# Both heads' scores in one product for the first two units: q stacked, k beside zeros

## The chip, the cores and the metric

The kernel runs on one core of a Trainium2 chip. The metric is device time in microseconds (us): three runs of the kernel before gave a median of 1116.27 us (1116.1 to 1117.86).

## The reference

Attention with two kinds of masks (heads 0 to 3 see 32 keys back, heads 4 to 7 every fourth of 128 back), and a gated feed-forward on the result, with RMS normalisation ahead of it. All is float32.

```
q, k, v: (8 batches, 8 heads, 576 positions, 64)
scores = q k^T / 8, masked by head; attn = softmax(scores) ; out = attn v
x = out as 4608 tokens x 512
xn = x / sqrt(mean(x^2) + 1e-6) * rms_g
y = (silu(xn w_gate) * (xn w_val)) w_out        w_gate, w_val: 512 x 1536, w_out: 1536 x 512
```

## The kernel before, in words

The 4608 tokens are worked off in 16 units of 288 (half a batch each). A unit has four pairs of heads (c = 0 to 3, heads 2c and 2c+1) and 14 bursts: three blocks of 96 queries for each of the first two pairs, four classes of 72 for the other two. A burst is a short chain: TensorE's scores of both heads (`scored`), VectorE's mask and maximum (`scores_max`, L384), ACT's exponentials (L395), sums, POOL's or VectorE's scaling (L411), TensorE's transposes (L487), ACT's copy (L467), TensorE's product with v (L496), ACT's copy into the unit's x (L428). The feed-forward of a unit is 12 groups of gate, value and output products (L650 in float32 for unit 0, L653 and L656 in three parts for the others).

Nothing is scheduled by hardware choice: each engine runs its instructions in the order in which they are written down. Tables of step numbers at the head of the file, and `later(dt, rank, fn)`, which puts a piece of work into a later step, set this order. Unit 0's attention has no other matrix work beside it; filler products (`busy`, L774) stand between its bursts. Unit 1's attention stands inside unit 0's feed-forward, and so on.

SP issues all transfers, in the order of the table ORDER at first: q and k of pairs 0 and 1, v, q and k of pair 2, the first two weight pieces, and so on. The weights come as 64-bit words and are turned into float32 in steps: a rebase on POOL or ACT (L166, L168), then shifts and ors on VectorE (L174, L177, L181). A ninth transfer waits until the first of the eight before it has landed, since eight counters (DMAHW0 to DMAHW7) serve all transfers in turn.

Units 0 and 1 (`u < NNAT`) work their scores in plain float32, with a contraction of 128 rows of which only 64 hold data. `zeros` makes, for each pair of heads, a tile of 128 partitions with q and k of one head beside q and k of the other; it fills partitions 64 to 127 with zeros (L262), and `load_qk` (L273) writes partitions 0 to 63 in one transfer. `scored` then has one product per head (L509). For the second unit's pairs 1 to 3 the zeros are written in later steps (table ZEROS) and the loads are issued in later steps (table SECOND). Unit 2 uses L509 too, with other tiles; from unit 3 on, L512.

## Time and profile before

| | |
|---|---|
| median of three runs | 1116.27 us |
| the profiled execution | 1116.57 us, of it 1114.8 us span |
| PE busy | 1102.5 us, 99% of the span |
| DVE, ACT, POOL busy | 60%, 64%, 61% |
| granted TensorE clock | 1.00 |
| L509, rows of scores | 168, from 5.1 to 152.7 us |
| L262, zeros | 13 on POOL, 3 on DVE, 538 to 680 ns each |

A float32 product shows as two rows, each with its weight load (PEld). PE is TensorE, DVE VectorE, ACT ScalarE, POOL GpSimd; a name with a q, such as SPq, is that engine's sequencer. In the chain of waits a row has start, length and what ran. In the timeline a row has start, length, engine, line, operation, output <- input, shape and how many; in brackets stands the engine's idle time before it, and what ended it. In the rows of groups the last columns are busy time in all and mean ns of one, then the idle time before them. In the rows of transfers the size of one and the median time from issue to landing stand last.

### The profile page before, as it was taken

How to read it: one execution, taken by the hardware profiler on the slowest of the kernel's cores; microseconds unless marked ns; L12 is line 12 of the kernel's file. 1: busy time of each engine (PE TensorE's matmuls, PEld its weight loads, DVE VectorE, ACT ScalarE, POOL GpSimd, SP SyncE). 2: the span in 40 equal slices, each digit the busy share in tenths (PEclk: the TensorE clock that was granted, in tenths of full speed). 3: DMA queues.
4: the chain of work that ended last, by engine and by line, in shares of the span. 5: the costliest groups of instructions: out<-in, count | busy, mean ns of one | idle time of the engine just before them, and what ended most of it. 6: DMA issues, size and time to landing. Idle time of an engine off the chain costs nothing.

```text
span 1114.8 us, 25463 instructions
## 1 busy us (share of the span) xinstructions
PE 1102.5 (99%) x8362; PEld 1076.9 (97%) x8362; DVE 670.9 (60%) x2734; ACT 708.8 (64%) x2579; POOL 674.7 (61%) x1154
## 2 busy tenths in 40 slices
PE   7999999999999999999999999999999999999998
PEld 5787999999999999999999999999999999999998
DVE  7889667656566564656656565665656656565312
ACT  6795676757576675767657576675757667575311
POOL 7423578756586665757657575675658657584211
PEclk9999999999999999999999999999999999999999
DMA  9665213212131121311212121131312212120000
GB/s 252 195 231 197 73 43 88 84 35 79 41 95 50 41 85 41 94 40 55 82 39 84 41 83 54 47 96 29 87 43 80 64 32 80 53 73 13 11 13 22
DMA packets 61542, 82.16 MB, mean 74 GB/s; under 512 B 7298, under 2 KB 41090, under 8 KB 61410
## 3 DMA queue, kind: packets, MB, share of 16 engines
q1 hardware_dynamic: 61410, 80.54, 24.4%
q8 instruction: 66, 1.08, 0.4%
q14 instruction: 66, 0.54, 0.2%
HBM read 71.08 MB, written 9.44 MB: 72 GB/s over the span
## 4 chain that ended last, share of the span: by engine, by line
PE 94%; POOL 2%; ACT 1%; DVE 1%; DMA 1%; issue 1%; SPq 0%; POOLq 0%; ACTq 0%; DVEq 0%
PE acc L656 17%; PE g L656 17%; PE v L656 17%; PE acc L653 9%; PE g L653 8%; PE v L653 8%; PE s L512 3%; PE o L500 3%; PE acc L650 2%; PE v L650 2%; PE g L650 2%; PE t L487 2%; PE o L501 1%; PE g L487 1%; PE o L496 1%; PE s L509 1%
## 5 line engine op out<-in xcount | busy, mean ns | idle before, releaser
L723 POOL TENSOR_TENSOR hlo<-th,hhi 128x288 fp32r<-128x288 f32 x179 | 145.7, 814 | 185.1 <-ACT hhi L722 169.9
L656 PE MATMUL acc<-hhi,lo 128*128 128x288 f32 x720 | 212.6, 295 | 0.0
L698 DVE SCALAR_TENSOR_TENSOR th<-th,g 128x288 f32<-128x288 f32 x180 | 81.8, 454 | 213.0 <-ACT pt L467 124.7
L395 ACT ACTIVATE t<-t,sum 96x128 f32<-96x128 f32 (+3 forms) x448 | 165.3, 372 | 33.5 <-DVE sum L384 32.0
L656 PE MATMUL g<-xhi,lo 128*128 128x288 f32 x612 | 180.3, 295 | 0.0
L656 PE MATMUL v<-xhi,lo 128*128 128x288 f32 x612 | 180.2, 294 | 0.0
L411 POOL TENSOR_SCALAR t<-t,sum 72x72 f32<-72x72 f32 (+3 forms) x414 | 152.2, 379 | 31.6 <-DVE sum L405 20.5
L693 ACT ACTIVATE th<-g 128x288 f32<-128x288 f32 x180 | 73.9, 411 | 151.3 <-PE g L487 59.0
L323 POOL TENSOR_TENSOR vlo<-vt,vhi 128x128 fp32r<-128x128 f32 x182 | 84.2, 463 | 116.7 <-ACT vhi L319 113.5
L656 PEld LDWEIGHTS acc<-hhi,lo 128*128 128x128 f32 x720 | 135.4, 188 | 0.0
L722 ACT CAST hhi<-th 128x288 fp32r<-128x288 f32 x180 | 77.8, 432 | 85.3 <-DVE th L711 84.7
L442 DVE TENSOR_TENSOR xraw<-o,xraw 64x72 f32<-64x72 f32 (+1 forms) x364 | 97.3, 267 | 42.0 <-ACT xraw L431 38.5
L656 PEld LDWEIGHTS v<-xhi,lo 128*128 128x128 f32 x612 | 115.1, 188 | 0.0
L656 PEld LDWEIGHTS g<-xhi,lo 128*128 128x128 f32 x612 | 115.1, 188 | 0.0
L711 DVE TENSOR_TENSOR th<-th,v 128x288 f32<-128x288 f32 x180 | 81.0, 450 | 54.7 <-PE v L656 53.0
L653 PE MATMUL acc<-hhi,hi_o 128*128 128x288 f32 x360 | 109.0, 303 | 0.0
L653 PE MATMUL g<-xhi,hi_g 128*128 128x288 f32 x357 | 106.8, 299 | 0.0
L656 PE MATMUL acc<-hlo,hi_o 128*128 128x288 f32 x360 | 106.4, 296 | 0.0
L431 ACT COPY xraw<-o 64x72 f32<-64x72 f32 (+1 forms) x364 | 95.5, 262 | 9.7 <-PE o L501 7.6
L353 POOL TENSOR_TENSOR ks<-qk,ks 128x288 fp32r<-128x288 f32 (+2 forms) x104 | 93.3, 901 | 3.1
L656 PE MATMUL g<-xlo,hi_g 128*128 128x288 f32 x322 | 95.1, 295 | 0.0
L362 POOL TENSOR_TENSOR qs<-qk,qs 64x288 fp32r<-64x288 f32 x104 | 84.2, 809 | 14.6 <-ACT qs L357 7.8
(188 smaller groups left out, 3522.2 us busy)
## 6 DMA issues: line engine op xcount, KB each, us to landing
qk<-in_qk_dram SPq DMA_DIRECT2D x60, 288.0 KB, 2.9
vt<-in_v_dram SPq DMA_DIRECT2D x196, 64.0 KB, 1.9
qk<-in_qk_dram SPq DMA_DIRECT2D x30, 352.0 KB, 3.0
out_dram<-ot SPq DMA_DIRECT2D x64, 144.0 KB, 1.9
qk<-in_qk_dram SPq DMA_DIRECT2D x30, 304.0 KB, 2.9
raw<-in_w_gate_dram SPq DMA_DIRECT2D x12, 512.0 KB, 5.7
raw<-in_w_val_dram SPq DMA_DIRECT2D x12, 512.0 KB, 5.5
raw<-in_w_out_dram SPq DMA_DIRECT2D x12, 512.0 KB, 4.2
```

Source lines behind the costliest of these rows:

```text
L323: G.tensor_tensor(out=vl, in0=vs.pop(b), in1=vh, op=ALU.subtract)
L353: ek.tensor_tensor(out=ks[:, 1, :nkt], in0=kr, in1=ks[:, 0, :nkt], op=ALU.subtract)
L362: eq.tensor_tensor(out=qs[D:], in0=qr[D:], in1=qs[D:], op=ALU.subtract)
L395: A.activation(out=t[:nq, a, :n], in_=t[:nq, a, :n], func=AF.Exp, scale=-1.0, bias=sm[:nq, a, 0:1], accum_out=sm[:nq, a, 1:2] if u or i % ...
L411: (V if u == 0 and (c, i) > (NC - 1, 0) else G).tensor_scalar(out=t[:nq, a, :n], in0=t[:nq, a, :n], scalar1=sm[:nq, a, 3:4], scalar2=1.0, ...
L431: A.copy(out=to[a * D:(a + 1) * D], in_=o[a * D:(a + 1) * D, (2 + a) * nq:(3 + a) * nq])
L442: V.tensor_tensor(out=to[rows], in0=o[rows, a * nq:(a + 1) * nq], in1=to[rows], op=ALU.add)
L653: PE.matmul(out, wh[:, cc, :], xh, start=start, stop=False)
L656: PE.matmul(out, w[:, cc, :], v, start=False, stop=stop and k == 1)
L698: V.scalar_tensor_tensor(out=t, in0=t, scalar=1.0, in1=g, op0=ALU.add, op1=ALU.mult)
L711: V.tensor_tensor(out=t, in0=t, in1=v_ps[:, :U], op=ALU.mult)
L723: (V if (u, j) == (NU - 1, NJ - 1) else G).tensor_tensor(out=lo, in0=t, in1=hi, op=ALU.subtract)
```

## The change

The tile of a pair of heads now has 288 columns of q and two blocks of k. Partitions 0 to 63 hold q of the first head and partitions 64 to 127 q of the second. The first block of k has the first head's k in partitions 0 to 63 and zeros below; the second has zeros in partitions 0 to 63 and the second head's k below. One product with q stacked as the stationary operand, and both blocks as the moving operand, gives both heads' scores side by side. The zeros cover k's columns alone. The load is three transfers: q and k of the first head (L274), k of the second (L275), q of the second (L276). The host's arrays are as before, and already hold q and k in both halves of the rows.

```diff
-        t = cst.tile([P, 2, U + KW], F32, tag=f"hi{4 * (u * NC + c)}", name=f"qk_{u}_{c}")
+        t = cst.tile([P, U + 2 * KW], F32, tag=f"hi{4 * (u * NC + c)}", name=f"qk_{u}_{c}")
+        ks = t[:, U:].rearrange("p (a k) -> p a k", a=2)
         def fill():
             for a, e in enumerate(engines):
-                e.memset(t[D:, a, :U + geometry(u, c)[2]], 0.0)
+                e.memset(ks[(1 - a) * D:(2 - a) * D, a, :geometry(u, c)[2]], 0.0)
...
-        heads[u, 2 * c], heads[u, 2 * c + 1] = t[:, 0], t[:, 1]
+        heads[u, c] = t[:, :U], ks
         return t

     def load_qk(u, c, t):
         nkt = geometry(u, c)[2]
-        nc.sync.dma_start(out=t[:D, :, :U + nkt],
-                          in_=qk_in[u, 2 * c:2 * c + 2, :D, :U + nkt].rearrange("a p n -> p a n"))
+        nc.sync.dma_start(out=t[:D, :U + nkt], in_=qk_in[u, 2 * c, :D, :U + nkt])
+        nc.sync.dma_start(out=t[D:, U + KW:U + KW + nkt], in_=qk_in[u, 2 * c + 1, D:, U:U + nkt])
+        nc.sync.dma_start(out=t[D:, :U], in_=qk_in[u, 2 * c + 1, D:, :U])
...
             sv = s_ps[:QB].rearrange("q (a t k) -> q a t k", a=2, t=2)
+            if q[0] < NNAT:
+                if a:
+                    return
+                qs, ks = heads[q[0], q[1]]
+                PE.matmul(sv[:nq, :, 0, :n], qs[:, qc:qc + nq], ks[:, :, kc:kc + n], start=True, stop=True)
+                return
             if q[0] < NEX:
```

On SP, at the start of the program, the order before was this (qk_0 to qk_3 are the tiles of unit 0's pairs, raw the weight pieces; what an instruction waits for stands in brackets):

```order
L273 DMA qk_0_103<-in_qk_dram 64x2x576
L273 DMA qk_1_106<-in_qk_dram 64x2x576
L280 DMA v_0_123<-in_v_dram 128x384
L273 DMA qk_2_109<-in_qk_dram 64x2x576
L154 DMA raw_126<-in_w_gate_dram 128x1024
L154 DMA raw_126<-in_w_val_dram 128x1024
L280 DMA v_1_129<-in_v_dram 128x384
L273 DMA qk_3_112<-in_qk_dram 64x2x576
L280 DMA v_3_132<-in_v_dram 72x512 [waits DMAHW0_49]
L280 DMA v_2_134<-in_v_dram 72x512 [waits DMAHW1_49]
L762 DMA gs<-in_rms_g_dram 128x4x1 [waits DMAHW2_49]
L154 DMA raw_137<-in_w_gate_dram 128x1024 [waits DMAHW3_49]
```

With the change SP starts so:

```order
L274 DMA qk_0_103<-in_qk_dram 64x576
L275 DMA qk_0_103<-in_qk_dram 64x288
L276 DMA qk_0_103<-in_qk_dram 64x288
L274 DMA qk_1_106<-in_qk_dram 64x576
L275 DMA qk_1_106<-in_qk_dram 64x288
L276 DMA qk_1_106<-in_qk_dram 64x288
L282 DMA v_0_127<-in_v_dram 128x384
L274 DMA qk_2_109<-in_qk_dram 64x576
L275 DMA qk_2_109<-in_qk_dram 64x288 [waits DMAHW0_49]
L276 DMA qk_2_109<-in_qk_dram 64x288 [waits DMAHW1_49]
L154 DMA raw_132<-in_w_gate_dram 128x1024 [waits DMAHW2_49]
L154 DMA raw_132<-in_w_val_dram 128x1024 [waits DMAHW3_49]
```

The first w_val moves from the sixth to the twelfth place and now waits for the landing of the fourth transfer; before, it waited for none. The second pair of weights moves from the places 12 and 13 to 20 and 21, where it waits for the first w_val (DMAHW3) and the second v (DMAHW4).

On TensorE, in unit 0's feed-forward with unit 1's attention in it, the order before was this (t and g are transposes of L487 or gate products of L650, o the product with v, s the scores):

```order
L487 MATMUL t_1_696<-ident,t_0_2_597 128x96 [waits DVE_49,PE_49]
L487 MATMUL t_1_696<-ident,t_0_2_597 128x96
L496 MATMUL o_0_1_697<-pt_0_1_650,v_0_144 128x192 [waits PE_49,Activation_49]
L650 MATMUL g_2_717<-xn_588,f_539 128x288 [waits DVE_49]
L650 MATMUL g_2_717<-xn_590,f_539 128x288
L650 MATMUL g_2_717<-xn_593,f_539 128x288
L650 MATMUL g_2_717<-xn_595,f_539 128x288
L487 MATMUL g_2_717<-ident,t_1_0_610 128x96 x2
L509 MATMUL s_2_0_722<-qk_2_119 72x104 [waits DMAHW7_49,DVE_49,Pool_49]
L509 MATMUL s_2_0_722<-qk_2_119 72x104 [waits Pool_49]
```

The same place with the change:

```order
L489 MATMUL t_1_692<-ident,t_0_2_596 128x96 [waits DVE_49]
L489 MATMUL t_1_692<-ident,t_0_2_596 128x96
L498 MATMUL o_0_1_693<-pt_0_1_647,v_0_154 128x192 [waits PE_49,Activation_49]
L658 MATMUL g_2_713<-xn_587,f_538 128x288 [waits DVE_49]
L658 MATMUL g_2_713<-xn_589,f_538 128x288
L658 MATMUL g_2_713<-xn_592,f_538 128x288
L658 MATMUL g_2_713<-xn_594,f_538 128x288
L489 MATMUL g_2_713<-ident,t_1_0_608 128x96 x2
L513 MATMUL s_2_0_718<-qk_2_119 72x2x104 [waits DMAHW3_49,DMAHW4_49,DVE_49,DMAHW5_49,PE_49,Pool_49]
```

Two products of scores are one of twice the columns; it waits for three transfers and for TensorE's own counter, which the transposes ahead no longer do. The order of the other work is unchanged on every engine.

## The prediction

> **What bounds the kernel now.** I read the busy times by stage first, because the change touches only the first two units of tokens, whose attention is over by 112 us. A row has the stretch and its length, then busy time and number of instructions of PE, PEld, DVE, ACT and POOL, the granted clock, the DMA share and GB/s.
>
> ```profile
> 0.00:5.00 5.00, 2.50 (x5) 1.49 (x5) 1.61 (x3) 1.58 (x2) 4.37 (x24) 1.00 0.55 126
> 5.00:45.00 40.00, 34.41 (x208) 26.37 (x209) 32.99 (x147) 27.72 (x110) 24.82 (x40) 1.00 0.92 240
> 45.00:112.00 67.00, 67.00 (x333) 53.92 (x332) 60.04 (x130) 50.69 (x144) 22.42 (x18) 1.00 0.60 211
> ```
>
> From 45 to 112 us TensorE is busy all 67.00 us: there only shorter matrix work shortens the run. Before 45 us it is idle for 2.50 + 5.59 us, and its busy time holds filler products (L774) that nobody waits for. There the chain of waits decides, which I read next, in that window.
>
> ```profile
> 0.73 0.73 SPq L273
> ...
> 4.07 7.11 DMA raw<-in_w_val_dram
> ...
> 11.33 1.11 POOL f L166
> 12.44 0.86 POOL t L411
> ...
> 32.04 0.70 POOL qk L262 x2
> ...
> 35.17 0.88 POOL rst L568
> ...
> 43.30 2.21 PE v L650 x8
> ```
>
> The chain starts in the DMA queue: the first pair of weight pieces is complete when w_val lands at 4.07 + 7.11 = 11.18 us, and POOL's rebase L166 starts on it at 11.33. Behind that instruction POOL holds the softmax scaling L411, for which TensorE's transposes wait. From there the chain runs over all four engines, with no slack that I can name, to 43.30, where TensorE becomes full. I therefore count a delay at 11.33 as a delay of the end, one for one.
>
> **The change, part by part.**
>
> *Products.* There are 28 bursts (14 in each of two units) with two products each, which become one with twice the columns and the same stationary width. Does a product cost its columns or its weight load? Three pieces of the chain from a stretch where TensorE has no gap, and one group of weight loads:
>
> ```profile
> 45.84 0.44 PE s L509 x4
> 46.27 1.94 PE acc L650 x8
> ...
> 50.84 0.36 PE s L509 x4
> L509 PEld LDWEIGHTS s<-qk x39: 141/143/165, 45.5 to 111.9; 128*72 128x72 f32 x32, 128*96 128x96 f32 x7
> ```
>
> A product is two rows here. The first four rows have 128 columns each: 0.44 / 512 = 0.86 ns a column. The last four have 104: 0.36 / 416 = 0.87. Weight products have 288: 1.94 / 2304 = 0.84. The rows of 104 columns follow each other every 90 ns although one weight load takes 143, so loads are overlapped and columns set the pace. Two rows of 256 columns cost 512 x 0.84 to 0.86 = 0.43 to 0.44 us against 0.44: 0 to 0.01 us a burst. About ten bursts (39 loads / 4) lie in the full stretch, a gain of 0 to 0.1 us; I take 0.1. Earlier, TensorE waits anyway.
>
> [...] The rows above grow by 0.08 us for 96 columns, 0.83 ns a column, which leaves nothing fixed to save.
>
> VectorE loses nothing by waiting for a whole burst, as it did so before: its first read started when the fourth row had ended (33.47 + 0.60 = 34.07), not after the second.
>
> ```profile
> 33.47 0.60 PE L509 MATMUL s<-qk 128*96 128x128 f32 x4
> 34.11 0.29 DVE L384 CUSTOM_DVE_ANT_0 t<-s,mask 96x128 f32<-96x128 f32 x1
> ```
>
> In many bursts the new product also waits for TensorE's own counter. What it waits for stands 5 to 14 products earlier, and the old order has such waits ahead of output products in the full stretch; I cost them at nothing. Without that cover each would cost about the drain behind a last row, 0.60 (the busy time of four rows, below) - 0.44 = 0.16 us, and ten of them 1.6.
>
> *Fills.* Each now leaves out q's columns.
>
> ```profile
> L262 POOL MEMSET qk<- 64x576 f32 x5 | 2.6, 573 | 0.1
> L262 POOL MEMSET qk<- 64x704 f32 x4 | 2.6, 679 | 0.1
> 8.02 1.36 POOL L411 TENSOR_SCALAR t<-t,sum 96x96 f32<-96x96 f32 x4 [1.96 <-DVE sum L384]
> 11.33 1.11 POOL L166 TENSOR_SCALAR f<-raw 128x1024 f32<-128x1024 f32 x1 [0.83 <-DVE sum L384]
> 17.83 1.13 POOL L166 TENSOR_SCALAR f<-raw 128x1024 f32<-128x1024 f32 x1 [0.28 <-DVE sum L405]
> 34.93 0.16 DVE L567 TENSOR_SCALAR rst<-rps 96x3 f32<-96x3 f32 x1
> 46.31 2.37 POOL L171 TENSOR_SCALAR raw<-raw 128x1024 f32<-128x1024 f32 x1 [7.65 <-issue]
> ```
>
> From 573 and 679 ns one column costs (679 - 573) / 128 = 0.83 ns and the rest 96, so 288 columns take 0.33 us and 320 take 0.36. The seven fills at the start save 1.7 us, in front of an idle 1.96 us ahead of 8.02; those of the last two tiles stand ahead of an idle 7.65. Both are worth nothing. The pair at 32.04 is on the chain and ends 0.47 us sooner. But POOL's L568 at 35.17 also needs VectorE's L567, which ends at 34.93 + 0.16 = 35.09. So this gains at most 0.08 us; I take 0.05.
>
> *Transfers.* One load of q and k becomes three: 16 more transfers, each issued on SP, six of them ahead of the first weight pair.
>
> ```profile
> 5.05 1.99 PE L509 MATMUL s<-qk 128*96 128x96 f32 x12 [0.18 <-DMA qk<-in_qk_dram]
> 2.80 0.59 SPq L273 DMA_DIRECT2D qk<-in_qk_dram  x1
> 3.43 0.59 SPq L154 DMA_DIRECT2D raw<-in_w_gate_dram  x1
> 4.07 0.43 SPq L154 DMA_DIRECT2D raw<-in_w_val_dram  x1
> 4.54 0.43 SPq L280 DMA_DIRECT2D v<-in_v_dram  x1
> 8.70 0.36 SPq L154 DMA_DIRECT2D raw<-in_w_gate_dram  x1
> 9.89 0.34 SPq L154 DMA_DIRECT2D raw<-in_w_val_dram  x1
> raw<-in_w_val_dram SPq DMA_DIRECT2D x1, 512.0 KB, 7.8
> DMA to landing us min/median/max: 3.6/6.4/10.0
> ```
>
> Issues follow each other every 0.63 us around a q load (2.80 to 3.43) and every 0.47 between plain ones (4.07 to 4.54). A transfer of 64 plain rows is nearest to the latter. The w_val issue is now the twelfth instead of the sixth: 0.73 (where the first issue starts) + 0.14 (it took 0.73, the third 0.59) + 11 x 0.47 = 6.0 us, and 7.8 by 0.63. It must also wait until the fourth transfer (half of the second load) has landed. The first whole load lands at about 5.0 now, just ahead of the first scores at 5.05, so I expect the fourth transfer near 6, which changes nothing.
>
> What is a later issue worth? The shortest time from issue to landing of a weight piece is 3.6 us, and this one takes 7.11: for 3.5 us it stands in line behind earlier bytes. The DMA share of 0.92 from 5 to 45 us says the same: engines are short, not issues. The bytes ahead of it do not change. So an issue up to 11.18 - 3.6 = 7.6 leaves the landing where it is; 6.0 is inside, 7.8 is outside. By 0.63, w_gate is issued at 7.2 and lands alone at 10.8; w_val, which now lands 1.3 us after it (3.43 + 6.4 = 9.8, the 6.4 from a row below, against 11.18), lands at 12.1, 0.9 us late. The other way, POOL stood idle for 0.83 us ahead of 11.33, which is all that an earlier landing can give. I take 0, with -0.8 and +0.9 as ends.
>
> The second pair was issued at 8.70 and 9.89 and landed at 9.89 + 7.8 = 17.7, just ahead of POOL's L166 at 17.83. Its issues now wait for the landings of the first w_val (11.2) and the second v (11.9): 11.9 + 3.6 = 15.5 is still 2.2 us early. If that cover is gone, POOL's next L411 and a transpose are late by what is missing.
>
> *Sum.* -0.1 (products) - 0.05 (the pair at 32.04) + 0 (transfers) = -0.15 us. The profiled execution took 1116.57 us (span 1114.8), 0.3 above the median of 1116.27. I predict 1116.2 for the median; this case's own range is 1115.1 to 1117.3.
>
> **Rivals.**
>
> *The line does not absorb the issues (slower).* If each of the six added transfers holds the line for one issue slot, and w_val still takes its 7.11 us from issue to landing, it lands 6 x 0.47 = 2.8 to 6 x 0.63 = 3.8 us later, POOL's L166 with it: 1119.0 to 1120.1. It decides from a landing past 13.4 us. For it: only eight transfers may be out at once, and these now hold fewer bytes, so the engines could run empty. Against it: 7.11 against 3.6, and the DMA share.
>
> *The loads get faster (a little faster).* Here q's loads are the slow ones:
>
> ```profile
> qk<-in_qk_dram SPq DMA_DIRECT2D x1, 288.0 KB, 5.9
> raw<-in_w_gate_dram SPq DMA_DIRECT2D x1, 512.0 KB, 6.4
> ```
>
> The third load, issued at 2.80, lands at 8.7, w_gate at 9.8, w_val at 11.18. So a piece of 512 KB adds 1.1 to 1.4 us to the line, at which rate 288 KB would add 0.7; but the three q loads and one v ahead of it (1056 KB, 2.7 us at that rate) needed until 8.7. If halves that go to different partitions move side by side, three loads save more than 0.8 us by w_val's landing, of which POOL can use 0.83, and 0.28 more ahead of 17.83: 1116.3 - 1.1 = 1115.2. Against it: the halves are transfers that follow each other, each to 64 partitions as before. [...]
>
> *Weight loads do cost (faster).* If each dropped load of 143 ns were exposed, ten bursts with two fewer would gain 2.9 us: 1113.4. Against it stand the 90 ns rows.
>
> **How the numbers follow.** The forecast has 0.74, the slower rival 0.13, faster loads 0.09, weight loads 0.04. A measurement here can tell about 0.2%, 2.2 us, from no change. The forecast and the faster loads lie inside (0.83), less 0.03 for their tails; so same 0.80, slower 0.13, faster 0.07 (weight loads and the tail below). The range that holds 8 in 10 takes in both ends of the transfers and the lower part of the slower rival: 1114.6 to 1118.6.
>
> **What would show it.** Right: w_val lands between 10.4 and 12.1 us and POOL's first L166 starts with it; TensorE's chain becomes full within 1 us of 43.30; a scoring product of 2x128 columns takes 0.43 to 0.44 us, one of 2x104 takes 0.35 to 0.36. Wrong: POOL idle for more than 3 us ahead of the first L166; gaps ahead of TensorE's scores after 45 us; or a chain from 11 to 43 us that shrinks or grows by itself, because POOL and VectorE meet at other places than now.

## The result, and the profile after

The changed kernel took 1119.72 us (median of nine executions, 1118.74 to 1123.7) against 1116.6 us before in the same comparison (1115.79 to 1119.89): a ratio of 1.0026, 95% interval 1.0014 to 1.0039. The forecast was 1116.2, and the range ended at 1118.6: the change costs about 3 us where none was forecast. The profiled execution of the changed kernel is its slowest, 1123.7 us with a span of 1121.9.

First the stages, as before: the stretch and its length, busy time and instructions of PE, PEld, DVE, ACT and POOL, the granted clock, the DMA share, GB/s. The kernel before, 5 to 8 us:

```profile
5.00:8.00 3.00, 2.95 (x20) 2.77 (x20) 1.73 (x14) 1.52 (x6) 1.06 (x2) 1.00 1.06 210
```

The changed kernel:

```profile
0.00:5.00 5.00, 2.63 (x7) 2.02 (x8) 0.89 (x3) 1.58 (x2) 4.01 (x25) 1.00 0.33 99
5.00:8.00 3.00, 3.00 (x11) 2.28 (x9) 1.97 (x16) 1.67 (x7) 0.23 (x1) 1.00 0.72 188
5.00:45.00 40.00, 35.04 (x152) 26.31 (x151) 26.32 (x128) 24.49 (x95) 21.49 (x38) 0.83 0.73 221
```

Two columns have moved: the DMA engines are less busy in the first 8 us (0.33 against 0.55, then 0.72 against 1.06), and the granted clock of 5 to 45 us is 0.83 instead of 1.00. The chain of waits of the changed kernel shows both:

```profile
5.66 0.60 SPq L275
...
6.30 0.59 SPq L276
...
6.94 0.58 SPq L154
...
7.57 5.04 DMA raw<-in_w_val_dram
...
12.76 1.10 POOL f L166
13.86 0.86 POOL t L413
...
14.77 0.71 PE t_first L489 x2
15.48 0.69 PE o L498 x2
16.17 0.48 PE s L513 x2
16.65 0.85 PE busy L782 x2
```

SP needs 0.56 to 0.60 us for each part of q and k, one after the other (0.47 for the one behind v), 0.62 to 0.64 from start to start. So w_val is issued at 7.57 us (before: 4.07) and lands at 7.57 + 5.04 = 12.61 (before: 11.18). POOL's rebase L166 starts on it at 12.76 (before: 11.33). From 14.77 on the chain stays on TensorE, where it was not before, and the filler products (`busy`, L782) are part of it: two of them take 0.85 us, 0.43 each.

The timeline of the changed kernel, start, length, engine, line, operation, output <- input, shape, and the idle time ahead in brackets:

```profile
12.76 1.10 POOL L166 TENSOR_SCALAR f<-raw 128x1024 f32<-128x1024 f32 x1 [2.46 <-DMA raw<-in_w_val_dram]
14.77 0.71 PE L489 MATMUL t_first<-ident,t 96*96 96x96 f32 x2 [2.74 <-POOL t L413]
49.41 2.21 PE L658 MATMUL v<-xn,f 128*128 128x288 f32 x8 [1.76 <-ACT pt L469]
```

POOL stood idle for 2.46 us until w_val was there (0.83 before) and TensorE for 2.74 us until POOL was done (1.05 before). TensorE is full from 49.41 on, before from 43.30. Between them stand stretches of half clock, here in rows of 1 us (the third number from the end is the clock):

```profile
14.00:15.00 1.00, 0.23 (x1) 0.15 (x1) 0.97 (x6) 0.00 (x0) 1.00 (x2) 0.69 1.16 227
15.00:16.00 1.00, 1.00 (x5) 0.84 (x5) 0.79 (x5) 0.00 (x0) 0.74 (x3) 0.50 0.96 360
...
20.00:21.00 1.00, 1.00 (x7) 0.92 (x5) 0.32 (x2) 0.16 (x2) 1.00 (x3) 0.50 1.06 214
21.00:22.00 1.00, 1.00 (x8) 0.84 (x7) 0.51 (x5) 0.96 (x5) 0.30 (x2) 0.90 1.04 208
```

A clock of 0.69 means that 0.62 of that 1 us ran at 0.50, so the fall is at 14.38; the 0.90 puts the rise at 21.20: 6.82 us. A second stretch of the same length begins near 31.4. This execution had two; the other eight executions of the changed kernel in this comparison have a mean clock of 0.998, as the profile of the cut load below has with a single stretch of 3.4 us, and take 1118.7 to 1120.4. I therefore took a second profile of the changed kernel among the experiments; that one fell on an execution with a clock of 1.00 throughout.

### The profile page after: what moved, and what is told of

Its sections match the earlier page's. It is cut to its first block, busy times and chain, and to the rows that moved or that the text cites. A ratio compares the mean times of both kernels' runs of the same rounds, so it can differ in the third digit from the quotient of the medians.

```text
span 1121.9 us, 25382 instructions
## 1 busy us (share of the span) xinstructions
PE 1108.0 (99%) x8306; PEld 1079.8 (96%) x8306; DVE 671.4 (60%) x2734; ACT 709.1 (63%) x2579; POOL 670.9 (60%) x1154
## 4 chain that ended last, share of the span: by engine, by line
PE 94%; DVE 1%; ACT 1%; POOL 1%; DMA 1%; SPq 1%; issue 1%; DVEq 0%; POOLq 0%; ACTq 0%
PE g L664 17%; PE acc L664 17%; PE v L664 16%; PE acc L661 9%; PE g L661 8%; PE v L661 8%; PE s L520 3%; PE o L502 3%; PE acc L658 2%; PE v L658 2%; PE g L658 2%; PE t L489 2%; PE o L503 1%; PE o L498 1%; PE g L489 1%; PE rps L568 1%
```

## The experiments

Each execution's record gives its mean granted clock. "At 1.00" below means 0.999 or 1.000 over the run, "lower" 0.998 or less. In five comparisons the kernel before was executed 159 times: 136 at 1.00 with a median of 1116.61 us, 23 lower with a median of 1119.03 (1117.65 to 1120.78). The ratio is to the kernel before in the same comparison, with its 95% interval.

| kernel | median (range), us | ratio | lower clock | median at 1.00 |
|---|---|---|---|---|
| cut load alone | 1118.20 (1117.78–1118.98) | 1.0013 (1.0004–1.0022) | 11 of 11 | – |
| changed + fillers | 1118.47 (1117.90–1119.94) | 1.0013 (1.0004–1.0022) | 2 of 11 | 1118.47 |
| changed, weights earlier | 1118.70 (1117.56–1120.47) | 1.0017 (1.0008–1.0026) | 7 of 11 | 1118.57 |
| joined product, one load | 1118.36 (1115.45–1120.29) | 1.0008 (0.9996–1.0019) | 7 of 11 | 1116.66 |
| before + fillers | 1117.17 (1116.57–1120.60) | 1.0004 (0.9996–1.0013) | 1 of 11 | 1117.14 |
| cut load + fillers | 1118.54 (1117.64–1122.43) | 1.0014 (1.0006–1.0023) | 4 of 11 | 1118.28 |
| one load + fillers | 1117.05 (1116.43–1120.16) | 1.0000 (0.9991–1.0008) | 1 of 12 | 1116.89 |
| parts on ACT + fillers | 1119.66 (1118.29–1120.75) | 1.0020 (1.0011–1.0028) | 2 of 11 | 1119.34 |
| changed, again | 1119.86 (1118.29–1123.46) | 1.0024 (1.0014–1.0034) | 8 of 12 | 1118.93 |
| two loads a pair | 1120.88 (1117.30–1125.87) | 1.0030 (1.0016–1.0043) | 8 of 12 | 1118.00 |
| six small issues | 1120.39 (1118.61–1121.54) | 1.0022 (1.0014–1.0031) | 11 of 11 | – |
| two loads + fillers | 1118.88 (1117.77–1121.17) | 1.0022 (1.0013–1.0031) | 3 of 11 | 1118.77 |
| one load, again | 1118.43 (1115.63–1121.42) | 1.0009 (0.9998–1.0020) | 5 of 11 | 1116.75 |
| parts on ACT | 1119.30 (1117.75–1121.28) | 1.0020 (1.0010–1.0029) | 4 of 11 | 1118.83 |
| six small issues + fillers | 1119.02 (1118.02–1121.74) | 1.0023 (1.0014–1.0032) | 8 of 11 | 1118.66 |
| changed + fillers, again | 1118.59 (1118.13–1121.19) | 1.0020 (1.0011–1.0028) | 5 of 12 | 1118.43 |
| the same, long fill | 1118.63 (1118.09–1119.16) | 1.0017 (1.0008–1.0025) | 0 of 11 | 1118.63 |
| one load + fillers + pause | 1116.63 (1115.31–1120.57) | 1.0003 (0.9991–1.0014) | 3 of 12 | 1116.61 |

What the profiles of these kernels show along the chain (us; "rst" is POOL's root of the sums of squares, L568 before and L576 with the change; "full" is where TensorE becomes full, from the first whole group of value products; "a stretch" is one of half clock):

| kernel | w_val issued | POOL's first L166 | square on DVE | rst on POOL | full | full − L166 |
|---|---|---|---|---|---|---|
| before | 4.07 | 11.33 | 0.45 | 0.87 | 43.30 | 31.97 |
| before + fillers | 4.07 | 11.35 | 0.45 | 0.87 | 43.55 | 32.20 |
| cut load (a stretch) | 7.57 | 12.63 | 0.45 | 0.87 | 44.94 | 32.31 |
| cut load + fillers | 7.58 | 12.73 | 0.45 | 0.87 | 44.53 | 31.80 |
| six small issues (a stretch) | 7.94 | 12.73 | 0.45 | 0.87 | 45.05 | 32.32 |
| six small issues + fillers (a stretch) | 7.94 | 13.17 | 0.45 | 0.87 | 45.85 | 32.68 |
| changed (two stretches) | 7.57 | 12.76 | 0.45 | 1.25 | 49.41 | 36.65 |
| changed, again | 7.58 | 12.23 | 1.05 | 1.24 | 44.70 | 32.47 |
| changed + fillers | 7.58 | 12.33 | 1.05 | 1.24 | 44.92 | 32.59 |
| changed + fillers, again | 7.57 | 12.79 | 1.04 | 1.25 | 45.36 | 32.57 |
| the same, long fill | 7.58 | 12.44 | 1.31 | 1.24 | 45.26 | 32.82 |
| changed, weights earlier (a stretch) | 5.15 | 9.85 | 1.05 | 1.24 | 44.03 | 34.18 |
| two loads a pair | 5.81 | 12.95 | 1.05 | 1.24 | 45.50 | 32.55 |
| two loads + fillers | 5.80 | 11.98 | 1.05 | 1.25 | 44.94 | 32.96 |
| parts on ACT | 5.58 | 13.03 | 1.05 | 1.24 | 45.59 | 32.56 |
| parts on ACT + fillers | 5.31 | 14.07 | 1.05 | 1.25 | 46.64 | 32.57 |
| one load | 3.06 | 10.69 | 0.97 | 1.24 | 43.48 | 32.79 |
| one load, again (a stretch) | 3.04 | 10.29 | 0.45 | 1.24 | 45.23 | 34.94 |
| one load + fillers | 3.06 | 12.17 | 0.97 | 1.24 | 44.70 | 32.53 |
| one load + fillers + pause (a stretch) | 3.05 | 10.79 | 0.45 | 1.24 | 46.48 | 35.69 |

### One part of the change at a time

The load alone is cut into three, into the old tile, with the old products and fills:

```diff
-        nc.sync.dma_start(out=t[:D, :, :U + nkt],
-                          in_=qk_in[u, 2 * c:2 * c + 2, :D, :U + nkt].rearrange("a p n -> p a n"))
+        nc.sync.dma_start(out=t[:D, 0, :U + nkt], in_=qk_in[u, 2 * c, :D, :U + nkt])
+        nc.sync.dma_start(out=t[:D, 1, U:U + nkt], in_=qk_in[u, 2 * c + 1, :D, U:U + nkt])
+        nc.sync.dma_start(out=t[:D, 1, :U], in_=qk_in[u, 2 * c + 1, :D, :U])
```

> The kernel before, with each of its loads of q and k for the first two units cut into the same three transfers as in the change, but into the old tile; zeros and products are the old ones. Theory A (late issues): the first w_val is issued near 7.6 us and lands near 12.6 instead of 11.2, POOL's first rebase starts near 12.8, TensorE stands idle for 2 us or more ahead of the transpose behind it, and its granted clock falls to half for some microseconds; the time is 2 to 4 us above the kernel before, as with the change. Theory B (the joined product or the new tile costs it): the time is within 1 us of the kernel before, whatever the landing does.

It took 1118.20 us, 1.6 more than before and less than the 2 to 4 of theory A, and TensorE was full at 44.94, 1.64 late. The cut accounts for about half of the loss, without the product.

The joined product alone: the host lays out a pair's q, both blocks of k and the zeros as one array, and the tile comes in one transfer to all 128 partitions, with no fills on the chip.

```diff
-        nc.sync.dma_start(out=t[:D, :U + nkt], in_=qk_in[u, 2 * c, :D, :U + nkt])
-        nc.sync.dma_start(out=t[D:, U + KW:U + KW + nkt], in_=qk_in[u, 2 * c + 1, D:, U:U + nkt])
-        nc.sync.dma_start(out=t[D:, :U], in_=qk_in[u, 2 * c + 1, D:, :U])
+        n = U + 2 * geometry(u, c)[2]
+        nc.sync.dma_start(out=t[:, :n], in_=qz_in[u, c, :, :n])
```

> The changed kernel with q stacked and k beside its zeros laid out by the host, so that a pair is one transfer to 128 partitions (432 KB instead of 288 in unit 0) and nothing is filled with zeros; products as changed. Theory A: w_val is issued by 4.1 us and lands at 10.5 to 11.5, the clock does not fall, the time is within 1 us of the kernel before, or up to 1 us below it. Theory B: it stays 2 to 4 us above. If the added zeros hold the line (50% more bytes at twice the rate), w_val lands no later than 11.5; if bytes count alone, three loads add 1.5 us and it lands near 12.5, with the loss of the change.

Its executions spread from 1115.45 to 1120.29 and seven of eleven had a lower clock; the four at 1.00 have a median of 1116.66, that of the kernel before. The joined product alone costs nothing that these four show, but it gains nothing either, although the weights land earlier:

```profile
10.69 1.12 POOL L166 TENSOR_SCALAR f<-raw 128x1024 f32<-128x1024 f32 x1 [0.61 <-DVE sum L376]
43.48 2.21 PE L648 MATMUL v<-xn,f 128*128 128x288 f32 x8 [1.77 <-ACT pt L459]
```

The DMA engines moved 204 GB/s in the first 5 us and 302 in 5 to 8, where the kernel before moved 126 and 210: 1.6 and 1.4 times as much, not the twice that the expectation put in. POOL starts 0.64 us sooner than before and TensorE is full 0.18 later. Some 0.8 us are lost on the way; the last experiments look for them.

The second profile of the changed kernel stood beside two of the later runs:

> The changed kernel once more, beside the two below. Theory (late w_val, then a granted clock that halves for one stretch of 3.4 us or two): w_val lands at 12.2 to 12.7 us, the profiled execution has a clock of 0.998, TensorE becomes full between 45.5 and 47.5 us (49.41 in the first profile, with a clock of 0.994), median 1119.3 to 1120.1. Rival (the 3.1 us of the first comparison were the chance of one chip): 1118.0 to 1118.6.

Median 1119.86, ratio 1.0024, so the loss is no chance of one chip. Of its profile, at a clock of 1.00:

```profile
12.23 1.11 POOL L166 TENSOR_SCALAR f<-raw 128x1024 f32<-128x1024 f32 x1 [1.97 <-DMA raw<-in_w_val_dram]
44.70 2.21 PE L658 MATMUL v<-xn,f 128*128 128x288 f32 x8 [1.77 <-ACT pt L469]
```

The expectation had TensorE full after 45.5 and a lower clock; this execution had neither, and w_val landed at 12.09, just outside.

### The granted clock: fillers over the gap

Eight more filler products in the step behind the gap that had grown from 1.05 to 2.74 us. They change nothing but TensorE's idle time.

```diff
-            busy(0 if n < 2 else BUSY[1] if n < nb + LAG - 1 else 1)
+            busy(0 if n < 2 else BUSY[1] + 8 * (n == 6) if n < nb + LAG - 1 else 1)
```

> The changed kernel with eight more filler products (0.21 us each at the full clock) behind the first score of the third pair, where TensorE stood idle for 2.5 us ahead of the transpose that waits for POOL. Landings stay as with the change. Theory A1 (idle time lowers the clock): the granted clock stays at 1.0 over 14 to 22 us and the time falls by 1 to 2 us against the change, to 1.0 to 2.0 us above the kernel before; what is left is the late landing, 1.4 us. Theory A2 (only the late landing counts, the clock is by chance): the time stays 3 us above the kernel before, or more, as the fillers add up to 1.7 us.

The changed kernel with them, its first transposes and its stage:

```profile
14.35 0.61 PE L489 MATMUL t_first<-ident,t 96*96 96x96 f32 x2 [0.67 <-POOL t L413]
...
5.00:45.00 40.00, 33.99 (x172) 24.27 (x170) 31.58 (x144) 26.12 (x102) 22.62 (x38) 1.00 0.77 229
```

The gap is 0.67, the clock stays at 1.00, and only 2 of 11 executions (5 of 12 in the repetition) were lower, where the changed kernel has 17 of 21. The median falls to 1118.47, 1.9 above the kernel before, as theory A1 had it. The control, and the parts with fillers:

> The kernel before with the same eight filler products in the same step as the run with fillers had (both follow the gap of 1.05 us ahead of the first transposes at 13.35 us). It is the control for the fillers. If fillers in that gap only hold the granted clock up, the median is 1116.2 to 1116.6 (before: 1116.61 in the first comparison), and the runs of 1117.65 to 1120.62 with a clock of 0.996 to 0.998 that the kernel before has in 4 of 33 are gone. If the fillers themselves hold the chain up (eight of 0.21 us are 1.7 us, more than the gap of 1.05), it is 0.5 to 0.7 us slower: 1117.1 to 1117.3.

The kernel before with the fillers took 1117.17: as in the rival there they hold its chain up by 0.3 to 0.4 us, and 1 of 11 executions was still lower.

> The load cut into three parts, old tile and old products, with the eight fillers. Theory (late issue, one for one): the clock stays at 1.00 and 1.3 to 1.5 us remain, 1117.9 to 1118.1. Rival (most of the 1.6 us that the cut alone cost was the clock's fall, whose record was 0.998 in ten of its eleven runs): 1116.9 to 1117.4.

Fewer lower clocks (4 of 11 instead of 11) and 1118.28 at 1.00: 0.2 above the theory's times, but 1.5 above the kernel before at 1.00 in that comparison (1116.75), the theory's upper end. What the cut alone costs is the late landing. Its one stretch of half clock (3.4 us, near 16 to 19.6) shows as 0.5 us between the first rebase and full (32.31 against 31.80), but hardly in the times: 1118.20 without fillers is 1.7 above the kernel before at 1.00 in its comparison (1116.49).

> The joined product from a tile that comes whole in one transfer (zeros included, laid out by the host), with the eight fillers. Without fillers its runs with a clock of 1.00 took 1115.45 to 1117.94 and those with 0.995 to 0.998 took 1117.03 to 1120.29. Theory (the joined product costs nothing, what was left was the clock): median 1115.8 to 1116.6, clock 1.00 in nearly all runs. Rival (the joined product costs by itself, by waits on TensorE's own counter or because VectorE starts later): 1117 to 1118 with a clock of 1.00.

1117.05, and 1116.89 at 1.00, with a spread of 1116.43 to 1118.35: between the two forecasts, and level with the kernel before plus fillers. Lower clocks became rare (1 of 12, without fillers 12 of 22 in two comparisons), but the clock is not all that scatters the executions of the one-load kernel: those at 1.00 without fillers lie between 1115.45 and 1119.02.

So fillers make the falls of the clock rarer (7 of 23 executions of the changed kernel, 17 of 21 without them), which makes idle time on TensorE one cause of them; whether a given execution has one is a matter of chance. Idle time of some length is not the only cause. In or behind gaps of 2.73 to 2.78 us the clock fell in the profiles of the changed kernel, the cut load and the six small issues, and behind gaps of 2.18 and 1.94 us, further on, in those of the weights earlier and of the six issues with fillers. But in the profiles of "one load, again" and of the pause it fell at 27.34 and 28.57 us, where TensorE's longest gaps in the ten microseconds before are 0.79 and 0.98 us; why it fell there stays open. The changed kernel's twelve executions when it ran again have 1118.93 at 1.00 (four) and 1120.05 lower (eight): 1.1 us.

The stretches lasted 6.8 and 3.4 us; what sets this length, no run shows. Nor does the length of a gap decide by itself: in the changed kernel the clock fell behind a gap of 2.74 us (in the cut kernel behind one of 2.73), and in the profile with two loads a pair, below, it held behind one of 2.94.

### What made w_val late: issues or the cut

Issues alone: the kernel before, with six transfers of 64 x 2 numbers into columns that nobody reads.

```diff
+        if u == 0 and c < 3:
+            for a in range(2):
+                nc.sync.dma_start(out=t[:D, a, U + nkt:U + nkt + 2], in_=qk_in[u, 2 * c + a, :D, :2])
```

> The kernel before with six more transfers of 64 x 2 numbers each (512 bytes) ahead of the first weight pair, two behind each of the first three loads of q and k, into columns that nobody reads. Theory (six issues are the price, whatever they carry): w_val is issued near 7.3 us and lands between 12.2 and 13.2; median 1117.8 to 1118.6. Rival (the line of bytes absorbs the issues as long as the large transfers stay whole, and the cut into small pieces was the price): w_val lands at 11.2 to 11.7, and the median is 1116.5 to 1117.1.

```profile
7.94 0.43 SPq L154 DMA_DIRECT2D raw<-in_w_val_dram  x1
12.73 1.10 POOL L166 TENSOR_SCALAR f<-raw 128x1024 f32<-128x1024 f32 x1 [2.57 <-DMA raw<-in_w_val_dram]
```

The landing is as late as in the changed kernel, with no byte moved elsewhere: six issues are enough. The median, 1120.39, was above the expected 1118.6; all eleven executions had a lower clock. With fillers:

> The kernel before with six small added transfers and the eight fillers: the price of six issues alone, with the clock held. Without fillers w_val landed at about 12.6 us, every run had a lower clock, and the median was 1120.39. Theory (landing 1.4 us late, one for one, the rest was the clock): clock 1.00 in most runs, median 1118.3 to 1118.9. Rival (the small transfers cost more than their issues, further on): 1119.5 to 1120.5 with a clock of 1.00.

1119.02, eight of eleven still lower, and 1118.66 in the three at 1.00, the theory's end. That is 2.2 us above the kernel before at 1.00 in that comparison (1116.45): more than the 1.4 of the landing, and the fillers' 0.3 to 0.4 explain only a part of the difference. In its profile, at a lower clock, POOL's first rebase starts at 13.17, 1.8 late, so the landing was later here than in the run without fillers.

Fewer issues, same bytes: k and q of the second head in one transfer in unit 0, so three added issues instead of six.

```diff
+        if nkt == U:
+            nc.sync.dma_start(out=both[D:, :, :U],
+                              in_=qk_in[u, 2 * c + 1, D:, :2 * U].rearrange("p (a n) -> p a n", a=2))
+            return
```

> The changed kernel, but k and q of the second head come in one transfer for unit 0: two issues a pair, so three added ahead of the first weight pair instead of six, with the same bytes to the same places. Theory (SP's issues feed the DMA engines too slowly, so each added issue delays the pair): w_val is issued near 5.8 us and lands at 11.6 to 12.0, half way between 11.18 and 12.6; median 1117.2 to 1118.4, the lower end if the granted clock holds. Rival (what delays it is the form of the transfers, with data for partitions 64 to 127 apart from those for 0 to 63): w_val still lands after 12.2 and the median stays within 0.3 us of the changed kernel's.

```profile
5.81 0.43 SPq L154 DMA_DIRECT2D raw<-in_w_val_dram  x1
...
12.95 1.10 POOL L166 TENSOR_SCALAR f<-raw 128x1024 f32<-128x1024 f32 x1 [2.68 <-DMA raw<-in_w_val_dram]
```

Issued 1.8 us earlier, it landed no earlier; that is the rival's landing, while the executions at 1.00 (1117.30, 1117.42, 1118.59, 1119.64) lie on both sides and the median, 1120.88, is above what either had. Again, with fillers:

> Two transfers a pair in unit 0 (three added issues), with the eight fillers that keep the granted clock up. In its first profile w_val was issued at 5.81 us and landed at 12.8, though the engines had moved as many bytes by 12 us as before the change. Theory A (with engines kept full, the landing differs from one execution to the next by what is taken ahead of it from later transfers): w_val lands at 11.4 to 12.0 in this profile, and the times with a clock of 1.00 spread over 1.5 us or more, the fastest near 1117.2. Theory B (two loads a pair delay it as much as three, always): it lands at 12.6 to 13.0 again, and the times lie together at 1118.2 to 1118.8.

```profile
5.80 0.43 SPq L154 DMA_DIRECT2D raw<-in_w_val_dram  x1
...
11.98 1.11 POOL L166 TENSOR_SCALAR f<-raw 128x1024 f32<-128x1024 f32 x1 [1.66 <-DMA raw<-in_w_val_dram]
```

Now w_val landed by 11.83, a microsecond sooner for the same issue: theory A, as is the spread at 1.00, 1117.77 to 1120.16. The median is no better than with six issues.

Four of the parts on ACT's queue, so that SP has eight issues up to w_val:

```diff
+        e = nc.scalar if u == 0 and c in (1, 2) else nc.sync
+        e.dma_start(out=t[D:, U + KW:U + KW + nkt], in_=qk_in[u, 2 * c + 1, D:, U:U + nkt])
+        e.dma_start(out=t[D:, :U], in_=qk_in[u, 2 * c + 1, D:, :U])
```

> The changed kernel with the eight fillers, and with four of the parts of pairs 1 and 2 issued on ACT's queue, so that w_val is issued after eight issues of SP instead of twelve, near 5.1 us. Theory (SP's issue pace sets the landing): w_val lands between 11.0 and 11.6 us, POOL's first L166 starts with it, median 1116.6 to 1117.2, against 1118.47 with all issues on SP. Rival (the transfers of 64 partitions themselves are slower, whoever issues them): w_val lands after 12.2 us and the median stays at 1118 to 1118.5.

> The changed kernel with four parts issued on ACT's queue, without fillers. With fillers w_val was issued at 5.31 us and landed at 13.92, and the clock-1.00 runs took 1118.3 to 1120.3. Theory A (that landing was chance): w_val lands at 11.5 to 13, median 1118.5 to 1119.7. Theory B (two queues served side by side hold it up always): 13.5 to 14.3, and a median of 1120 to 1121.5 with the clock's falls.

The chain of the first, then of the second:

```profile
5.31 8.61 DMA raw<-in_w_val_dram
```

```profile
5.58 7.30 DMA raw<-in_w_val_dram
```

Landings at 13.92 and 12.88, medians 1119.66 and 1119.30: the earlier issue buys nothing, against the theory of the first run; its rival had the landing, but a median more than 1 us too low. In the second run both numbers are those of theory A, so the first landing was in part chance.

The one-load kernel a second time:

> The joined product with q, k and zeros in one transfer a pair, again. Its first profile had w_val at 10.55 us, the same transfers with fillers on TensorE had it at 12.02. Theory A (chance of the execution): any value from 10.5 to 12.1, and times with a clock of 1.00 from 1115.4 to 1118. Theory B (something in the two programs differs, such as TensorE's own reads): 10.4 to 10.7 again, and times with a clock of 1.00 within 0.5 us of each other.

POOL's first rebase started at 10.29 without waiting for a transfer, so w_val had landed by then, earlier than both theories had it; three profiles of the same transfers (10.55, 12.02, before 10.29) differ by more than 1.7 us, and its executions at 1.00 spread from 1115.63 to 1119.02. With w_val issued at 3.04 to 3.06 in all three, the landing is not fixed by the issue.

The weights earlier in the order of loads (ahead of the first v and of pair 2's q and k):

```diff
-ORDER = [(0, 0, "q"), (0, 1, "q"), (0, 0, "v"), (0, 2, "q"), (0, 0, "w"), (0, 1, "v"), (0, 3, "qv"), (0, 2, "v"),
+ORDER = [(0, 0, "q"), (0, 1, "q"), (0, 0, "w"), (0, 0, "v"), (0, 2, "q"), (0, 1, "v"), (0, 3, "qv"), (0, 2, "v"),
```

> The changed kernel with the first weight pair issued ahead of the first v and of the third pair's q and k. Theory A: w_val is issued near 5.3 us and lands near 10.2, so POOL's first rebase starts by 10.7; the third pair's k lands near 12, which holds its score back by up to 1 us; the time is within 1.5 us of the kernel before. Theory B (product or tile): the time stays 3 us above the kernel before.

POOL's first rebase came at 9.85, but the second waited 1.65 us for its w_val until 18.31, and TensorE was full at 44.03; median 1118.70, 2.1 above the kernel before, which neither theory had. What the one pair gains, the other transfers lose.

### The square on VectorE

In the second table, among the profiles without a stretch of half clock, every kernel with the joined product is full 32.5 to 33.0 us after POOL's first rebase, and every one with the old product 31.8 to 32.2. The two groups differ at one place, where POOL and VectorE meet twice. Before:

```profile
32.04 1.14 POOL L262 MEMSET qk<- 64x608 f32 x2
...
33.72 0.45 DVE L454 TENSOR_TENSOR sq<-sq,sq 128x288 f32<-128x288 f32 x1
33.75 1.42 POOL L166 TENSOR_SCALAR f<-raw 128x1024 f32<-128x1024 f32 x1
34.23 0.67 PE L560 MATMUL rps<-inv,sq 128*96 128x2 f32 x6 [0.16 <-DVE sq L454]
...
35.17 0.87 POOL L568 TENSOR_TENSOR rst<-rst,mhalf 96x3 f32<-96x3 f32 x1
35.20 0.71 DVE L174 TENSOR_SCALAR f<-f 128x1024 uint32<-128x1024 uint32 x1
```

With the change (second profile):

```profile
32.50 0.77 POOL L263 MEMSET qk<- 64x320 f32 x2
...
33.76 1.12 POOL L166 TENSOR_SCALAR f<-raw 128x1024 f32<-128x1024 f32 x1
...
34.15 1.05 DVE L456 TENSOR_TENSOR sq<-sq,sq 128x288 f32<-128x288 f32 x1
35.25 0.67 PE L568 MATMUL rps<-inv,sq 128*96 128x2 f32 x6 [0.76 <-DVE sq L456]
...
36.03 0.68 DVE L174 TENSOR_SCALAR f<-f 128x1024 uint32<-128x1024 uint32 x1
36.20 1.24 POOL L576 TENSOR_TENSOR rst<-rst,mhalf 96x3 f32<-96x3 f32 x1 [1.31 <-DVE rst L575]
```

Before, VectorE's square started 0.03 us ahead of POOL's third rebase; the square took 0.45 and the rebase 1.42. With the change POOL comes first. Counted from the first rebase, POOL's third now starts 0.89 us sooner (33.75 - 11.33 = 22.42, 33.76 - 12.23 = 21.53), VectorE's square only 0.47 (22.39, 21.92). The pair of zero fills, 0.77 instead of 1.14 us, is 0.37 of POOL's gain; the rest no run separates. The rebase now takes 1.12, and the square ends 0.32 after it: 34.15 + 1.05 = 35.20 against 33.76 + 1.12 = 34.88. TensorE's sums of squares wait for the square.

These 0.6 us of waiting are not the loss. Before, the chain ran over POOL's rebase, which ended at 35.17, and POOL went straight on to `rst`; VectorE's part of it had been ready 0.08 us earlier. With the change the rebase is done at 34.88 and `rst` waits for VectorE. Counted from the first rebase it starts at 35.17 - 11.33 = 23.84 before and at 36.20 - 12.23 = 23.97 now: 0.13 us later. And it takes 1.24 us instead of 0.87. Both together are the 0.50 us by which the stage grew (32.47 - 31.97). What differs beside `rst` is VectorE's shift L174: before it started 0.03 us behind `rst`, now 0.17 ahead of it. From the start of `rst` to full it is 8.13 us in all six profiles with the old product, and 8.50 or 8.51 in all fourteen with the joined one, also where the square took 0.45. Waiting alone does not lengthen `rst`: in the next unit of the kernel before it stands behind an idle time of 3.34 us (at 101.17 us) and takes 0.87. That L174's head start lengthens it is the reading that is left; no run moved L174 alone.

To test the part of the fills I lengthened one fill of that pair to 704 columns (the added ones are read by nobody), on the base of the kernel with fillers:

```diff
+                if (u, c, a) == (1, 1, 1):
+                    e.memset(t[:D, U + KW:2 * U + 2 * KW], 0.0)
+                    continue
```

> The changed kernel with the eight fillers, again, as the base for the next run. TensorE's sums of squares (six rows, rps) should wait 0.7 to 0.8 us for VectorE's square, which takes 1.0 to 1.1 us there; median 1118.2 to 1118.8.

> The same, but one of the two zero fills of unit 1's pair 1 runs over 704 columns instead of 320 (into columns that nobody reads), so that the pair takes about as long as before the change (1.09 against 1.14 us; 0.77 with the change). Theory (the shorter fills let POOL's rebase L166 start ahead of VectorE's square, which then takes 1.05 us instead of 0.45): POOL's L166 starts after VectorE's square, the square takes 0.45, the sums of squares wait 0.15 to 0.2, TensorE is full 31.8 to 32.2 us after POOL's first L166 instead of 32.5 to 33.0, and the median is 0.4 to 0.6 us below the run with the short fills. Rival (it is the joined product that makes VectorE late): the square still takes 1.0, the same median or 0.3 longer by the longer fill.

The base has the rows of the second table. The long fill:

```profile
33.19 0.68 POOL L264 MEMSET qk<- 64x704 f32 x1
...
34.33 1.11 POOL L166 TENSOR_SCALAR f<-raw 128x1024 f32<-128x1024 f32 x1
34.45 1.31 DVE L459 TENSOR_TENSOR sq<-sq,sq 128x288 f32<-128x288 f32 x1
35.81 0.67 PE L571 MATMUL rps<-inv,sq 128*96 128x2 f32 x6 [1.02 <-DVE sq L459]
```

My condition was missed by 0.12 us: POOL still came first. But the square shows what it does: begun 0.12 behind the rebase instead of 0.39, it takes 1.31 instead of 1.04, and ends at 35.76, again 0.32 behind the rebase's end (35.44). It seems to wait for the rebase and not to run beside it. TensorE is full 32.82 us after the first rebase instead of 32.57, and the median at 1.00 is 0.2 higher. The gain that was expected did not come; the rival's fixed 1.0 is out too, and VectorE is not late by itself, as its square starts sooner after the first rebase than before the change (22.01 here, 21.92 above, 22.39 before). And the version with one load, with three fills of unused columns on POOL at that place:

```diff
+        if (u, c) == (1, 1):
+            def fill():
+                for n in (480, 480, 96):
+                    G.memset(t[D:, U + 2 * nkt:U + 2 * nkt + n], 0.0)
+            later(ZEROS[0], 9.7, fill)
```

> The joined product with one load a pair and eight fillers, and on POOL three fills of columns that nobody reads (480, 480 and 96 columns, about 1.15 us) where the kernel before has the fills of unit 1's pair 1. Theory: the square takes 0.45 again and TensorE is full 31.8 to 32.2 us after POOL's first L166; median 1116.2 to 1116.8 with a clock of 1.00, 0.4 to 0.6 below the same without them (1116.89 with a clock of 1.00), so level with the kernel before or 0.3 faster. Rival: as without, 1116.8 to 1117.2.

Its median is 1116.63, and 1116.61 at 1.00 (nine, 1115.31 to 1118.52), against 1116.46 of the kernel before in that comparison: level, ratio 1.0003 (0.9991 to 1.0014). Its profiled execution had the clock fall, so that the square (0.45) came behind the rebase anyway; the place is not shown at a clock of 1.00. That the pause brings 0.3 us (1116.89 without, in another comparison) is therefore not shown. No version beat the kernel before.

## Why the prediction was wrong

**The issues (wrong, the first cause).** The step that failed is "A transfer of 64 plain rows is nearest to the latter", which chose 0.47 us an issue and w_val at 6.0. Measured: 0.56 to 0.60 a part, 0.62 to 0.64 from start to start, w_val issued at 7.57. The other end was the right one: "by 0.63" gave an issue at 7.8 and a landing at 12.1, 0.9 late; the profiles have 12.09 to 12.64, 0.9 to 1.5 late. The reason behind the choice failed with it: "engines are short, not issues" was read from the DMA share of 5 to 45 us. In 5 to 8 us, where the first weights stand in line, a pair's 288 KB in three issues of 0.64 us are 154 GB/s, less than the 210 GB/s that the engines moved there before, and their share fell from 1.06 to 0.72. The six small issues show that the issues suffice. What remains open is why w_val, issued at 5.3 to 5.8 us with fewer issues, landed at 11.8 to 13.9 all the same: with the engines kept busy the landing moved by about a microsecond or more between two profiles of the same transfers, and nothing I ran says which transfer goes ahead of which.

**The slower rival** had the right mechanism (the line does not absorb the issues) and too large a size: it needed a landing past 13.4. That its 1119.0 to 1120.1 hold the measured 1119.72 is luck: it counted 2.8 to 3.8 us of landing, where 0.9 to 1.5 came, and neither the stage behind nor the clock, which brought the rest.

**One for one (right).** A delay of POOL's first rebase is a delay of the end: in the profiles of the second table without a stretch of half clock the first rebase lies between 10.69 and 14.07 us, 3.4 us apart, and the time from it to full stays within 31.8 to 33.0. Profiles in which half clock held the chain are longer, and so is the run with the weights earlier, where the second pair took over.

**The fills (wrong, the second cause).** "The pair at 32.04 is on the chain and ends 0.47 us sooner" was bounded by "this gains at most 0.08 us", since `rst` also needs VectorE's L567, and a gain of 0.05 was taken. The pair took 0.37 us less, and POOL came to its rebase ahead of VectorE's square instead of behind it. The end of L567, which the bound took as fixed, moved with that: from 35.09 - 11.33 = 23.76 us after the first rebase to 36.12 - 12.23 = 23.89. And `rst` took 1.24 instead of 0.87: a loss of 0.5 us in place of a gain of 0.05. Whether shorter fills alone turn the order is not shown: the long fill missed it by 0.12 us, and the one-load kernel, which has no fills there, has the same order at a clock of 1.00. The prediction named POOL and VectorE meeting at other places among what would prove it wrong, but put no price on it. The row was there: DVE's square, 0.03 us ahead of a rebase that took 1.42 instead of 1.11.

The profiles show both orders, and in both the instruction that starts second takes longer than in the other order. Behind the square by 0.03 to 0.05 us, the rebase took 1.39 to 1.42 us (ahead of it 1.11 or 1.12); behind the rebase by 0.12 to 0.46, the square took 0.97 to 1.31 (otherwise 0.45). What makes it longer, no run shows.

**The products (right, and worth nothing).** A product of 2x128 columns was forecast at 0.43 to 0.44 us, one of 2x104 at 0.35 to 0.36. The chain of the changed kernel's second profile, in the full stretch:

```profile
47.24 0.43 PE s L513 x2
...
52.24 0.35 PE s L513 x2
```

From TensorE's full point to the end of the span it is 1071.0 to 1072.5 us with the joined product and 1071.5 to 1071.8 with the old one: the 0.1 us is below what can be seen. So the fast rival (weight loads exposed) is out. The waits on TensorE's own counter, put at nothing, cost nothing: TensorE is busy all 67.00 us from 45 to 112 in the second profile too.

**Faster loads (not seen).** That halves for different partitions move side by side was the author's assumption, and no run shows it. In the order of loads of the change, no profile with three transfers a pair has w_val landing before 12.09.

**The transfers of the second pair (right).** Its issues move to 12.6 and 13.4 us in the first profile, and POOL's second rebase at 19.59 waits for nothing. In the cut kernel, though, it waited 0.38 us for the second w_val, which landed at 13.45 + 5.61 = 19.06 us and not near the estimated 15.5: the cover of 2.2 us was used up.

**The clock (missing).** No term of the sum and no rival held a change of the granted clock. It is 0.8 to 0.9 us of the median: 1119.72 and 1119.86 over all, 1118.93 at 1.00.

**The sum as it came.** The landing, 0.9 to 1.5 us, and the stage of the square and `rst`, 0.5, are 1.4 to 2.0 us; the changed kernel lies 1.9 to 2.0 above the kernel before when both run at 1.00 (1118.93 against 1117.02, 1118.43 with fillers against 1116.46). The falls of the clock bring most of the rest of the 2.5 to 3.1. One part stays open. In the second profile the two terms make the 1.40 us at full (44.70 against 43.30), but from there to the end it is 1072.3 us against 1071.5; 0.54 of this is an idle stretch of TensorE at 467.60, in a later unit. Eight of the fourteen profiles with the joined product have such a stretch near there (0.14 to 0.86 us), none of the six with the old product.

## What to carry to other kernels

Read whether transfers or issues are short in the very microseconds in which the transfer in question stands in line, not over a stage (here the DMA share of 5 to 45 us was 0.92, and six small issues still made POOL's first rebase 1.4 us late), and cost an issue by rows of the same shape issued back to back (0.64 us here, not 0.47); splitting one early load into three can cost more than the matrix work it serves (here a landing 0.9 to 1.5 us later, for products that gained at most 0.01 us a burst). A gap that grows on TensorE can have a second price, the clock behind it (here a gap of 2.74 us instead of 1.05, and a lower clock in 17 of 21 executions), and filler work over the gap shows that price (7 of 23). Before calling a shorter instruction free, look at what its engine does next, which instruction of another engine it then overtakes, and how long both take in the new order (here a pair of fills shorter by 0.37 us, and a `rst` of 1.24 us instead of 0.87).

## What the runs showed of the hardware

- The mean granted clock was below 0.999 in 17 of 21 executions of the changed kernel, 11 of 11 with the cut alone, 12 of 22 with one load and 23 of 159 of the kernel before. In the seven profiles that caught a fall the clock halved for 3.4 or 6.8 us at a time. In three of them this was in or behind a TensorE gap of 2.7 to 2.8 us, in two behind gaps of 1.9 to 2.2, in two others with no gap above 1 us in the ten microseconds before; behind one of 2.94 it did not fall. In the changed kernel's first profile, where the fillers themselves became the chain at 0.43 us each, two stretches of 6.8 us cost 4.2 us on the way from POOL's first rebase to full (49.41 - 12.76 = 36.65 against 32.47); in the cut kernel one of 3.4 us cost 0.3 to 0.5 there (32.31 against 31.97 and 31.80).
- VectorE's square of 128x288 elements took 0.45, 0.97 to 1.05 or 1.31 us, by how early POOL's rebase had started; each long one ended 0.30 to 0.32 us behind the rebase.
- POOL's `rst` of 96x3 elements took 0.86 to 0.87 us, and 1.24 to 1.25 in the fourteen places where VectorE's shift of 128x1024 elements had started 0.16 to 0.17 us ahead of it.
- SP needed 0.57 to 0.60 us for an issue with 64 rows of 288 or 576 numbers behind another such, and 0.58 to 0.60 where each row is two numbers long: between these its price did not fall with the bytes.
